# Group 4's second layer in seven products, three load buffers in turn, and late spreads in a score bank

## The chip, the cores and the metric

The kernel runs on one NeuronCore of a Trainium2 chip. The metric is device time in microseconds (us) of one execution; the profile's own times start at the first instruction of the span. Engines are called by their names: TensorE (PE in the profile) multiplies matrices, VectorE (DVE), ScalarE (ACT) and GpSimd (POOL) do elementwise work, and SyncE (SP) issues most of the transfers. 16 DMA engines move the data.

## The reference

Two steps are computed, over a batch of 8, 8 heads, 576 positions and a head width of 64. First a Nystrom attention with 32 landmarks for each head, then a two-layer network on the 512 channels with its own normalization.

```python
q_lm, k_lm = means of q and k over 18 neighbouring positions     # 32 landmarks
A, Bm, C = softmax(q k_lm'), softmax(q_lm k_lm'), softmax(q_lm k')
Z = Bm' / (norm1(Bm) * norminf(Bm));  6 times: Z = 2 Z - Z Bm Z
x = A Z C v                                                      # [8*576, 512]
out = x + relu(normalized(x) * g @ w1) @ w2                      # 512 -> 2048 -> 512
```

The 4608 rows of x make 36 blocks of 128, and four blocks make a group, so that the network runs over nine groups of 512 rows (0 to 8).

## The kernel before, in words

**Two streams on TensorE.** The attention goes batch by batch: first batches 0 and 1, then four sets, (2), (3, 4), (5, 6) and (7). Each set is a `Coming` object (L510), which loads q, k and v by units of four heads into staging buffers, casts them to fp16 on GpSimd, turns them on VectorE and adds up landmarks. `attention2` (L660) is a generator with a yield after each step: scores of k, products with v, six iterations for Z, and then the rows, one block of x each. The network is another generator, `mlp` (L958). `fill(n)` (L1046) advances it by n yields, so n matmuls of 512 columns, or n pairs of matmuls of 256 columns. The plan `steps` (L1150) holds for each attention step of each set how many yields of the network follow it, how many casts, and how many preparation jobs (a turn, a landmark sum, or a spread) of the next set. The loop at L1155 carries this out. Every engine keeps the order in which the program issues its instructions, so an instruction that waits holds up those behind it on its engine. That is true of SyncE's queue of transfers as well.

**Normalization.** When a block of x is complete, `block_done` (L746) has its mean formed, its squares summed on ScalarE (`square`, one per attention step) and the block centred on GpSimd (`center`, L789), then turned by a transposing transfer into xnT, which the first layer reads. For groups below `G_FAST` (L45, 5) only the mean is taken off before the first layer, and 1/deviation is applied at the end, on VectorE, with the sum of x and the second layer in a buffer `ot`. For groups from `G_FAST` on, 1/deviation is applied before the first layer (`normalize`, L773, block by block), so that the second layer's result can be added straight to x.

**Second layer.** Below `G_FAST`, each of a group's four blocks takes sixteen matmuls of 512 columns into one bank. From `G_FAST` on, the 512 x 2048 by 2048 x 512 product is cut into 2 x 2 parts and done in seven products (Winograd's form of Strassen's) of sixteen matmuls with 256 columns each (`second_layer`, L870). It needs four mixes of w2's parts (`mixes_of_w2`, L857, on GpSimd) and four of the hidden layer's parts (`mix_of_h`, L946, and one inside `second_layer`, on VectorE). The first product is copied out by ScalarE and added three times by GpSimd; the others are collected two to a bank and added to x by VectorE.

**Buffers.** The staging pool `stage` (L58) has six buffers that are handed out in rotation to the loads; the four w2 mixes and two h mixes take all six once the loads are done. PSUM pools are `ps1` (one bank: iterations and small products), `ps2` (two buffers for scores, products with v, and rows) and `psM` (three banks: the network, and the landmark spreads psl of sets before batch 7). `mout` (L253) has four output buffers `ot`.

`prepare` (L1111) keeps three loads staged and not yet cast: after each cast it issues the next load. In set (2), step 9, three further loads are issued.

Of the kernel before, what the change touches and what calls it, by code (L numbers as in the profile page):

```python
# [16 lines left out]
P = 128  # L17
# [3 lines left out]
def kernel(  # L21
# [23 lines left out]
    G_FAST = 5  # L45
# [36 lines left out]
    def load(src, b, u, queue):  # L82
        t = stage.tile([P, 2, NJ, D], FP32, name="stg", tag="stg")
        keep(queue.dma_start(
            out=t[:],
            in_=src[b, 4 * u:4 * u + 4].rearrange("(r e) (t j) d -> (e t) r j d", e=2, j=NJ)))
        return t
# [14 lines left out]
    def load_turned(src, b, u, queue):  # L102
        t = stage.tile([P, 2, NJ, D], FP32, name="stg", tag="stg")
        rows = src[b, 4 * u:4 * u + 4].rearrange("(r e) (t j) d -> e t r j d", e=2, j=NJ)
        for half in range(2):
            keep(queue.dma_start(out=t[ts(half, 64), :, :, :], in_=rows[1 - half]))
        return t
# [401 lines left out]

    class Coming:  # L510
# [31 lines left out]
        def load(self, i, queue=nc.sync):  # L542
            nm, w = self.parts[i]
            b, u = self.units[w]
            src = {"q": q, "k": k, "v": v}[nm]
            self.stg[i] = (load_turned if nm == "v" and u % 2 == 1 else load)(src, b, u, queue)
# [54 lines left out]
        def spread(self, y):  # L601
            part = self.part.pop(y)
            late = self.bs[0] >= 7
            psl = (ps1 if late else psM).tile([P, 2, 8, LM], FP32, name="psl",
                                              tag="p1" if late else "pm")
            for half in range(2):
                MM(psl[:, half, :, :].rearrange("p k c -> p (k c)"),
                   spread16[:, half, :, :, :].rearrange("p e a w -> p (e a w)"),
                   part[:].rearrange("p n w r l x -> p (n w r l x)"))
            lm = asm.tile([P, 8, 2, LM], FP16, name="lm", tag="lm", bufs=3)  # L610
            scalar.copy(lm[:].rearrange("p k h c -> p h k c"), psl[:])
            for i, nm in enumerate(("q", "k")):
                for x in range(2):
                    self.lm[nm, 2 * y + x] = lm[:, ds(4 * i + 2 * x, 2), :, :].rearrange(
                        "p r h (l x) -> p r (h l) x", x=2)
# [130 lines left out]
    def block_done(j):  # L746
        g, u = divmod(j, 4)
        if g >= G_FAST:
            mean_of(j, dve)
            squares.append((at[0] + -4, lambda: normalize(j)))  # L750
            return
        if g == 0:
            mean_of(j, dve)
            center(j, scalar if u % 2 == 0 else dve)
        elif g == 1:
            mean_of(j, dve)
            later.append(lambda: center(j, scalar))
        else:
            later.append(lambda: mean_of(j, pool))
            later.append(lambda: center_in_turn(j))  # L760
        squares.append((at[0], lambda: square(j)))
        if u == 3:
            if g == 1:
                later.append(lambda: ln_ready.add(1))
            squares.append((at[0], lambda: deviations(g)))
# [7 lines left out]
    def normalize(j):  # L773
        g, u = divmod(j, 4)
        square(j)
        if u == 0:
            lnvs[g] = mstat.tile([P, 4], FP32, name="lnv", tag="lnv")
            rstds[g] = mstat.tile([P, 4], FP32, name="rstd", tag="rstd")
        act(lnvs[g][:, u:u + 1], variances[g][:, u:u + 1], AF.Ln, bias=eps_ln[:],
            scale=1.0 / DM)  # L780
        act(rstds[g][:, u:u + 1], lnvs[g][:, u:u + 1], AF.Exp, scale=-0.5)
        center_in_turn(j)
# [70 lines left out]
    w2_mix, h_mix = [], []  # L853
# [3 lines left out]
    def mixes_of_w2():  # L857
        for i in range(4):
            w2_mix.append(stage.tile([P, HK, HN], FP16, name=f"w2mix{i}", tag="stg"))
        for i in range(2):  # L860
            h_mix.append(stage.tile([P, HK, HN], FP16, name=f"hmix{i}", tag="stg"))
        t1, t2, t3, t4 = [t[:] for t in w2_mix]
        for o, a, b, op in ((t1, w12, w11, ALU.subtract), (t3, w22, w12, ALU.subtract),
                            (t2, t3, w11, ALU.add), (t4, w21, t2, ALU.subtract)):
# [4 lines left out]

    def second_layer(g, hT, mixed):  # L870
        t1, t2, t3, t4 = [t[:] for t in w2_mix]
        h11, h12 = hT[:, 0:HK, 0:256], hT[:, HK:MCH, 0:256]
        h21, h22 = hT[:, 0:HK, 256:], hT[:, HK:MCH, 256:]
        s1, s2, s3, s4 = mixed
        x = [x_blk.pop(4 * g + u) for u in range(4)]

# [3 lines left out]
        last = g == NGRP - 1  # L880

        def product(to, left, right, first=True, by_k=False):
            order = [(i, k) for i in range(2) for k in range(HK)]
            if by_k:
                order = [(i, k) for k in range(HK) for i in range(2)]
            for n, (i, k) in enumerate(order):
                apart = isinstance(to, list)
                MM(to[i][:] if apart else to[:, i, :], left[:, k, ts(i, P)], right[:, k, :],
                   start=first and (n == 0 or apart and k == 0), stop=k == HK - 1, skip=True)
                if n % 2 == 1 and n < 15:  # L890
                    yield True

        def add(engine, half, col, t, us=(0, 1)):
            for i in us:
                o = x[2 * half + i][:, ts(col, HN)]
                engine.tensor_tensor(out=o, in0=t[i][:] if isinstance(t, list) else t[:, i, :],
                                     in1=o, op=ALU.add)

        pa = bank("psp1")
        yield from product(pa, h11, w11)  # L900
        p1 = mout.tile([P, 2, HN], FP32, name="p1", tag="ot")
        scalar.copy(p1[:], pa[:])
        for half, col in ((0, 1), (1, 1), (1, 0)):
            add(pool, half, col, p1)
        yield True
        pb = bank("psp6")
        yield from product(pb, s2, t2, by_k=True)
        add(dve, 0, 1, pb)
        yield True
        yield from product(pa, h12, w21, False)  # L910
        add(dve, 0, 0, pa)
# [3 lines left out]
        for k in range(0, HK, 4):  # L915
            dve.tensor_tensor(out=s4[:, k:k + 4, :], in0=h12[:, k:k + 4, :],
                              in1=s2[:, k:k + 4, :], op=ALU.subtract)
        yield True
        yield from product(pb, s3, t3, False)
        add(dve, 1, 1, pb)  # L920
        yield True
        pc = ([psM.tile([P, HN], FP32, name="psp5", tag="pm"),
               ps1.tile([P, HN], FP32, name="psp5", tag="p1")] if last else bank("psp5"))
        yield from product(pc, s1, t1)
        add(dve, 1, 1, pc)
        yield True
        yield from product(pb, h22, t4, False)
        add(dve, 1, 0, pb)
        for u in (2, 3):
            store(4 * g + u, x[u], ts(0, DM), last)  # L930
        yield True
        c = product(pc, s4, w22, False)
# [3 lines left out]
        if last:  # L936
            add(dve, 0, 1, pc, (0,))
            store(4 * g, x[0], ts(1, HN), True)
        for _ in c:
            yield True  # L940
        add(dve, 0, 1, pc, (1,) if last else (0, 1))
# [4 lines left out]
    def mix_of_h(hT, mixed, m):  # L946
        s1, s2, s3, _ = mixed
        h11, h21, h22 = hT[:, 0:HK, 0:256], hT[:, 0:HK, 256:], hT[:, HK:MCH, 256:]
        k0, k1 = {11: (0, 4), 13: (4, 6), 14: (6, 7), 15: (7, 8)}[m]
        n = ds(k0, k1 - k0)  # L950
        dve.tensor_tensor(out=s1[:, n, :], in0=h21[:, n, :], in1=h22[:, n, :], op=ALU.add)
        dve.tensor_tensor(out=s2[:, n, :], in0=s1[:, n, :], in1=h11[:, n, :], op=ALU.subtract)
        if m == MCH - 1:
            for k in range(0, HK, 4):
                dve.tensor_tensor(out=s3[:, k:k + 4, :], in0=h11[:, k:k + 4, :],
                                  in1=h21[:, k:k + 4, :], op=ALU.subtract)

    def mlp():  # L958
        for g in range(NGRP):
# [18 lines left out]
            else:  # L978
# [11 lines left out]
                for m in range(MCH):  # L990
# [7 lines left out]
                    if g >= G_FAST:  # L998
                        if m == 0:
                            while not h_mix:  # L1000
                                yield False
                            mixed = [h[:] for h in h_mix] + [hT[:, 0:HK, 256:],
                                                             hT[:, HK:MCH, 0:256]]
                        if m - 1 in (11, 13):
                            mix_of_h(hT, mixed, m - 1)
                        elif m == MCH - 1:
                            mix_of_h(hT, mixed, 14)
                            mix_of_h(hT, mixed, 15)
# [127 lines left out]
    n = 0  # L1136
# [15 lines left out]
    steps += [[(12, 1, 0), (14, 1, 1), (16, 1, 1), (16, 1, 1)] + 6 * [(9, 1, 1)] + [(10, 1, 1)] + 10 * [(8, 1, 1)]]  # L1152
    steps += [[(15, 0, 0), (18, 0, 0)] + 6 * [(12, 0, 0)] + [(12, 0, 0)] + 5 * [(12, 0, 0)]]
    mixing = mixes_of_w2()
    for c, after, plan in zip(sets, sets[1:] + [None], steps):  # L1155
        while c.jobs:
            prepare(c, 1, 1)
            fill(5 if c is sets[1] else 8)
        for n, ((count, casts, jobs), _) in enumerate(zip(plan, attention2(c.bs, c))):
            for _ in range({(2, 9): 3}.get((c.bs[0], n), 0)):  # L1160
# [6 lines left out]
            if c in sets[2:] and not sets[-1].casts:  # L1167
# [39 lines left out]
```

## Time and profile before

| what | value |
|---|---|
| median of three runs | 319.52 us (317.84 to 319.77) |
| profiled execution, its own time | 318.94 us |
| its span | 317.2 us |
| mean granted TensorE clock | 0.991 |
| TensorE busy | 305.1 us (96%) |
| VectorE, ScalarE, GpSimd busy | 179.0, 161.0, 161.4 us |
| DMA engines' mean share by the core's loads and stores (queue q1) | 54.4% |
| time from issue to landing of a q load (median) | 7.4 us |

The profile is of one execution. In it a matmul's end is modelled, so that consecutive matmuls overlap in the timeline; the chain of waits and the starts give their pace. "idle before <- releaser" in brackets behind an instruction is the time that its engine stood still before it and what ended this; "issue" means that nothing in the profile ended it. In a row of busy times by stretch, each engine has its busy time and the number of its instructions, then come the granted clock (1.00 is full), the DMA share and GB/s. In names, psh is the first layer, pso a second layer in the plain form, psp one in seven products, psec and psea scores, pscv products with v, psn an iteration, psl a spread, psy a row block.

### The profile page before, as it was taken

How to read it: one execution, taken by the hardware profiler on the slowest of the kernel's cores; microseconds unless marked ns; L12 is line 12 of the kernel's file. 1: busy time of each engine (PE TensorE's matmuls, PEld its weight loads, DVE VectorE, ACT ScalarE, POOL GpSimd, SP SyncE). 2: the span in 40 equal slices, each digit the busy share in tenths (PEclk: the TensorE clock that was granted, in tenths of full speed). 3: DMA queues.
4: the chain of work that ended last, by engine and by line, in shares of the span. 5: the costliest groups of instructions: out<-in, count | busy, mean ns of one | idle time of the engine just before them, and what ended most of it. 6: DMA issues, size and time to landing. Idle time of an engine off the chain costs nothing.

```text
span 317.2 us, 8388 instructions
## 1 busy us (share of the span) xinstructions
PE 305.1 (96%) x3424; PEld 173.3 (55%) x3424; DVE 179.0 (56%) x487; ACT 161.0 (51%) x329; POOL 161.4 (51%) x218
## 2 busy tenths in 40 slices
PE   7889999999999979999999999999999999999994
PEld 7557764443444434544454445445854784685583
DVE  3667239868695215899276337756634860561372
ACT  3476853479227741267536646776038706505600
POOL 4389878919995794573003938900900360040050
PEclk9999999999999989999999999999999999999998
DMA  7999999779997994571087004340054016005013
GB/s 278 390 388 386 387 389 264 258 206 333 214 290 156 390 226 107 105 243 28 3 222 174 0 2 90 71 76 0 3 118 83 0 31 154 19 0 132 2 25 110
DMA packets 38862, 50.35 MB, mean 159 GB/s; under 512 B 17572, under 2 KB 18088, under 8 KB 38824
## 3 DMA queue, kind: packets, MB, share of 16 engines
q1 hardware_dynamic: 38504, 49.43, 54.4%
q8 instruction: 27, 0.44, 0.6%
q10 hardware_dynamic: 320, 0.39, 0.4%
q14 instruction: 11, 0.09, 0.1%
HBM read 36.70 MB, written 9.44 MB: 145 GB/s over the span
## 4 chain that ended last, share of the span: by engine, by line
PE 80%; DVE 8%; DMA 7%; issue 2%; POOL 1%; SPq 0%; ACT 0%; DVEq 0%
PE psh L75 39%; PE pso L75 16%; PE psp L75 16%; DMA stg<-in_k_dram 5%; DVE part L69 3%; DMA wstg<-in_moe_w_ch_dram 2%; PE psy L75 2%; PE psn L75 2%; DVE xblk L69 2%; PE pscv L75 2%; DVE xT L69 1%; DVE ot L69 1%; PE psec L75 1%; PE psea L75 1%; PE psl L75 0%
## 5 line engine op out<-in xcount | busy, mean ns | idle before, releaser
L75 PE MATMUL psh<-xnT,w 128*128 128x512 f16 (+1 forms) x640 | 136.2, 360 | 0.1
L69 ACT ACTIVATE hT<-psh 128x512 f16<-128x512 f32 x144 | 84.3, 599 | 78.1 <-PE psh L75 77.6
L75 PEld LDWEIGHTS <-w 128*128 128x128 f16 x640 | 59.0, 98 | 57.3 <-issue 4.2
L75 PEld LDWEIGHTS <-hT 128*128 128x128 f16 x640 | 61.2, 98 | 35.5 <-issue 2.1
L75 PE MATMUL pso<-w,hT 128*128 128x512 f16 x320 | 77.2, 382 | 0.0
L69 POOL TENSOR_TENSOR xblk<-p,xblk 128x256 f32<-128x256 f32 x24 | 17.3, 758 | 62.4 <-ACT p L69 62.4
L69 POOL CAST nat<-stg 128x1152 f16<-128x1152 f32 x28 | 31.6, 1148 | 14.8 <-DMA stg<-in_q_dram 13.2
L69 ACT ACTIVATE junk<-xblk,negm 128x512 f16<-128x512 f32 x36 | 25.9, 719 | 21.4 <-POOL negm L69 13.8
L69 POOL TENSOR_SCALAR xn<-xblk,negm,rstd 128x512 f16<-128x512 f32 x16 | 13.6, 859 | 43.8 <-ACT rstd L69 34.6
L69 DVE SCALAR_TENSOR_TENSOR xblk<-psy,rcpd 128x512 f32<-128x512 f32 (+1 forms) x40 | 27.6, 691 | 1.8
L69 DVE SCALAR_TENSOR_TENSOR st<-st,psn 128x128 f16<-128x128 f16 (+2 forms) x36 | 11.4, 316 | 30.0 <-PE psn L75 30.0
L69 DVE TENSOR_TENSOR xblk<-psp,xblk 128x256 f32<-128x256 f32 x48 | 18.2, 418 | 16.2 <-PE psp L75 16.1
L75 PE MATMUL psp<-w,hT 128*128 128x256 f16 x192 | 23.4, 273 | 0.0
L69 POOL CAST natv<-stg 128x1152 f16<-128x1152 f32 x16 | 18.3, 1164 | 7.4 <-DMA stg<-in_v_dram 7.2
L69 DVE TENSOR_TENSOR hmix<-hT 128x256 f16<-128x256 f16 (+2 forms) x16 | 6.8, 424 | 25.6 <-ACT hT L69 25.5
L69 DVE STREAM_TRANSPOSE xT<-nat 128x576 uint32<-128x576 uint32 x24 | 18.5, 769 | 0.0
L69 DVE TENSOR_REDUCE part<-xT 128x32 f16<-128x576 f16 x26 | 18.3, 744 | 0.1
L69 DVE SCALAR_TENSOR_TENSOR ot<-pso,rstd,xblk 128x512 f32<-128x512 f32 x20 | 14.9, 747 | 5.2 <-PE pso L75 5.0
L69 DVE RECIPROCAL rcpd<-psy 128x8 f32<-128x8 f32 (+1 forms) x40 | 8.1, 202 | 16.5 <-PE psy L75 16.0
L75 PE MATMUL psy<-zcbd,ea 128*128 128x260 f16 (+1 forms) x80 | 15.6, 276 | 0.7 <-DVE zcbd L69 0.5
L75 PE MATMUL psp<-w2mix,hT 128*128 128x256 f16 x128 | 15.5, 273 | 0.0
L75 PE MATMUL psp<-w2mix,hmix 128*128 128x256 f16 x128 | 15.3, 273 | 0.0
(116 smaller groups left out, 324.2 us busy)
## 6 DMA issues: line engine op xcount, KB each, us to landing
stg<-in_q_dram SPq DMA_DIRECT2D x16, 576.0 KB, 7.4
stg<-in_k_dram SPq DMA_DIRECT2D x16, 576.0 KB, 7.3
wstg<-in_moe_w_ch_dram SPq DMA_DIRECT2D x16, 512.0 KB, 7.0
stg<-in_v_dram SPq DMA_DIRECT2D x10, 576.0 KB, 8.9
out_dram<-ot SPq DMA_DIRECT2D x40, 128.0 KB, 2.7
stg<-in_v_dram SPq DMA_DIRECT2D x12, 288.0 KB, 10.8
out_dram<-xblk SPq DMA_DIRECT2D x26, 128.0 KB, 2.3
xnT<-xn SPq DMA_TRANSPOSE x28, 2.5
```

The source lines that it names most:

```text
L69: return lambda *args, **kw: keep(getattr(self.engine, op)(*args, **kw))
L75: keep(nc.tensor.matmul(o, l, r, start=start, stop=stop, tile_position=(rb, cb), skip_group_check=(skip or cb != 0)))
```

## The change

`G_FAST` becomes 4, so group 4 is normalized before its first layer and its second layer takes seven products as well. Its means are formed on GpSimd.

The seven products are put in another order, with three banks. The first product is no longer copied out: VectorE adds it from its bank (pa), then the product with s2 is collected on top of it, added to x, and the product with h21 on top of these, added to x twice. The second product has bank pe, which is used again for the fifth; the third and the last share bank pc. In group 4 the second reading of pa is a copy by ScalarE, added by GpSimd.

The first w2 mix is formed in place in w12, by VectorE, in group 4's first layer; three mixes are left on GpSimd, started in set (3, 4), step 16, and then one piece of two chunks per attention step. Two of the h mixes are formed in place in the hidden layer; the other two lie in the four output buffers, in halves.

Loads of sets (5, 6) and (7) go to three fixed staging buffers in turn. Spreads of these sets use a score bank of `ps2`. Groups 4, 6, 7 and 8 take their deviations together, after the fourth square, and are then centred; group 5 block by block as before.

In the plan, set (2) issues two further loads at step 9 instead of three. Before set (3, 4), each preparation job is followed by six yields instead of five. In set (5, 6), an iteration is followed by six instead of nine, the step after it by eight instead of ten, and each row by twelve instead of eight.

```diff
-    G_FAST = 5
+    G_FAST = 4
...
-    def load(src, b, u, queue):
-        t = stage.tile([P, 2, NJ, D], FP32, name="stg", tag="stg")
+    def load(src, b, u, queue, t=None):
+        t = t or stage.tile([P, 2, NJ, D], FP32, name="stg", tag="stg")
...
+            t = None
+            if self.bs[0] >= 5:
+                if len(ring) < 3:
+                    ring.append(stage.tile([P, 2, NJ, D], FP32, name="ring", tag="stg"))
+                    ring_at[0] = len(ring) - 1
+                t = ring[ring_at[0]]
+                ring_at[0] = (ring_at[0] + 1) % 3
+            self.stg[i] = (load_turned if nm == "v" and u % 2 == 1 else load)(
+                src, b, u, queue, t)
...
-            late = self.bs[0] >= 7
-            psl = (ps1 if late else psM).tile([P, 2, 8, LM], FP32, name="psl",
-                                              tag="p1" if late else "pm")
+            late = self.bs[0] >= 5
+            psl = (ps2 if late else psM).tile([P, 2, 8, LM], FP32, name="psl",
+                                              tag="p2" if late else "pm")
...
         if g >= G_FAST:
+            if g in (4,):
+                later.append(lambda: mean_of(j, pool))
+                squares.append((at[0], lambda: normalize(j)))
+                return
...
         square(j)
+        if g not in (5,):
+            if u == 3:
+                deviations(g)
+                for i in range(j - 3, j + 1):
+                    center_in_turn(i)
+            return
...
+    def last_mix_of_w2(k):
+        dve.tensor_tensor(out=w12[:, k:k + 2, :], in0=w12[:, k:k + 2, :],
+                           in1=w11[:, k:k + 2, :], op=ALU.subtract)
...
+        pa = bank("pspa")
         yield from product(pa, h11, w11)
+        add(0, 0, pa)
         yield True
+        pe = bank("pspe")
+        yield from product(pe, h12, w21)
+        add(0, 0, pe)
+        mix_less(h12, s2)
         yield True
+        pc = ([psM.tile([P, HN], FP32, name="pspc", tag="pm")[:],
+               ps1.tile([P, HN], FP32, name="pspc", tag="p1")[:]] if last else bank("pspc"))
+        yield from product(pc, s1, t1)
+        add(1, 1, pc)
+        yield True
+        yield from product(pa, s2, t2, False)
+        if g in (4,):
+            p6 = mout.tile([P, 2, HN], FP32, name="p6", tag="ot")
+            scalar.copy(p6[:], pa[:])
+            add(0, 1, p6, engine=pool)
+        else:
+            add(0, 1, pa)
+        yield True
+        yield from product(pe, h22, t4)
+        add(1, 0, pe)
...
+        yield from product(pa, h21, t3, False)
+        for u in (0, 1):
+            add(1, 1, pa, (u,))
+            add(1, 0, pa, (u,))
+            store(4 * g + 2 + u, x[2 + u], ts(0, DM), last)
         yield True
-        c = product(pc, s4, w22, False)
+        c = product(pc, h12, w22, False)
...
-                        if m - 1 in (11, 13):
-                            mix_of_h(hT, mixed, m - 1)
-                        elif m == MCH - 1:
-                            mix_of_h(hT, mixed, 14)
-                            mix_of_h(hT, mixed, 15)
+                            mixed = [[mout.tile([P, HK // 2, HN], FP16, name="hmix", tag="ot")[:]
+                                      for _ in range(2)] for _ in range(2)]
+                        if g == G_FAST and m in (2, 4, 6, 8):
+                            last_mix_of_w2(m - 2)
+                        if m in (12, 14, 15):
+                            mix_of_h(hT, mixed, m)
...
-    steps += [[(12, 1, 0), (14, 1, 1), (16, 1, 1), (16, 1, 1)] + 6 * [(9, 1, 1)] + [(10, 1, 1)] + 10 * [(8, 1, 1)]]
+    steps += [[(12, 1, 0), (14, 1, 1), (16, 1, 1), (16, 1, 1)] + 6 * [(6, 1, 1)] + [(8, 1, 1)] + 10 * [(12, 1, 1)]]
...
-            fill(5 if c is sets[1] else 8)
+            fill(6 if c is sets[1] else 8)
...
-            for _ in range({(2, 9): 3}.get((c.bs[0], n), 0)):
+            for _ in range({(2, 9): 2}.get((c.bs[0], n), 0)):
...
-            if c in sets[2:] and not sets[-1].casts:
+            if (c.bs[0], n) >= (3, 16):
```

## The prediction

> **What bounds the kernel now.** I read the page's first part, then the busy times by stretch, the waits of TensorE, and its timeline.
>
> ```profile
> PE 305.1 (96%) x3424; PEld 173.3 (55%) x3424; DVE 179.0 (56%) x487; ACT 161.0 (51%) x329; POOL 161.4 (51%) x218
> ```
>
> TensorE is the bound; the others are half idle. From 60 us to the end of the last product, its waits are only these (who, in us, times, longest):
>
> ```profile
> PE psn L75 <- issue: 1.8, 1, 1.8
> PE psl L75 <- DVE part L69: 0.9, 1, 0.9
> PE psn L75 <- ACT lm L69: 0.7, 1, 0.7
> ```
>
> So a change can gain only by giving TensorE less work or by removing these three stops. The chain of waits gives the price of the work: after 260 us it is TensorE alone, a first layer (psh) and a second layer in seven products (psp), in turn (start, length):
>
> ```profile
> 260.70 13.81 PE psh L75 x64
> 274.52 12.23 PE psp L75 x112
> ```
>
> A matmul of 512 columns takes 13.81/64 = 0.216 us, one of 256 columns 12.23/112 = 0.109 us. The largest stop is odd: it falls inside a group of sixteen psn matmuls that are all ready, and slow matmuls follow it (timeline of TensorE; busy times by stretch: PE busy and count, clock, DMA share, GB/s).
>
> ```profile
> 113.36 1.25 PE L75 MATMUL psh<-xnT,w 128*128 128x512 f16 x5
> 114.54 0.23 PE L75 MATMUL psn<-st 32*32 32x64 f16 x5
> 116.53 0.26 PE L75 MATMUL psn<-st 32*32 32x64 f16 x11 [1.76 <-issue]
> 116.72 2.05 PE L75 MATMUL psh<-xnT,w 128*128 128x512 f16 x5
> ```
> ```profile
> 106.00:114.00 8.00, 8.00 (x179) 1.00 1.06 331
> 114.00:116.00 2.00, 0.77 (x8) 1.00 1.01 266
> 116.00:118.00 2.00, 1.47 (x15) 0.76 1.08 205
> 118.00:120.00 2.00, 2.00 (x21) 0.50 1.01 221
> 120.00:122.00 2.00, 2.00 (x25) 0.89 0.83 194
> 122.00:124.00 2.00, 2.00 (x26) 1.00 0.06 22
> ```
>
> The stop comes while the DMA engines are full. Six loads of 576 KB (for batches 5 and 6, unit 1 of q to unit 0 of v; below q1, v0 and so on) are issued between 99.8 and 103.4 us; loads issued then land after 4.6 to 11.8 us. The instructions' DMA queue, which the page calls q8, moves a packet of 16 KB starting near 99.3, 106.3, 113.8, 121.0 and 130.5 us: never closer than 7 us while the queue is full, and TensorE resumes after the one at 113.8 (33.5% of 16 engines in a quarter of a us, so over a us long). I read the stop as TensorE out of instructions behind queued loads.
>
> [...]
>
> **The change, part by part.** The profiled execution took 318.94 us (span 317.2 and 1.7 around it), 0.58 below the median of 319.52; the sum is made on 318.94.
>
> A. Group 4's second layer: 64 matmuls of 0.216 (13.81) become 112 of 0.109 (12.23). All on the path: **-1.58**. The other groups keep 112.
>
> B. Three load buffers in turn. The six buffers let SyncE run up to six loads ahead. With three, load n waits for the cast of load n-3. Following Pool with its own rows (cast 1.15, sums after each q cast 3.0): q1, k2, k3 go out near 100, q2 near 104, then one load each 1 to 4 us, the last (k0 of batch 7) near 120 instead of 112. One to three are queued instead of six, and Pool has cast v1 near 120 (before: 121.3), since Pool, not the transfers, then sets the pace. [...] and TensorE not run dry. The stop is 1.76; the slow clock costs 0.81 (psh x5: 1.99 instead of 1.18), 0.10 (psn) and 0.67 (pso x5: 1.85 instead of 1.18). Between 0 (engines still full) and -3.3; I take **-3.3**. SyncE's waits: behind the waiting loads stand store 8 and the transposes of block 13, not ready before 124.
>
> C. Six matmuls instead of five in each of seven turns before (3,4)'s scores. DVE is busy without a gap from 88 to 95.7 there, and TensorE waits 0.92 at psl. Six more matmuls before psl are 1.3: **-0.9** (between -0.9 and 0).
>
> D. Landmark spreads move to the score banks: the psn that waited for the copy of psl out of the single ps1 bank loses its wait, **-0.7**. The score banks are free for over 1 us at those places.
>
> E. Group 4's normalization moves: the four blocks are centred together after their deviations at step 0 of (5,6), and xnT 16 to 19 follow there. From the first psec of (5,6), counted as zero: ACT's exponentials end at 2.3, square and deviations at 3.5, four centres of 0.77 on Pool at 6.7; SyncE issues store 13 (1.1) at 4.2 and four transposes of 1.22, the last at 9, landed (2.8) at 11.7. TensorE wants them after 44 psh/pso matmuls (9.5), psec, gram and two pscv (3.2): 12.7. Hidden with 1 us of cover; **+0.1** (0 to 2).
>
> F. Mixes of w2: twelve on Pool instead of sixteen, started at step 16 of (3,4), so that they (1.12 each) stand between batch 7's casts. By the same clock, Pool reaches the end of q1's cast and sums at 22.0. DVE reaches the turn of q1 near 21, at its end of step 6, and waits; behind it stand st of iteration 3 and the sums of spread 7. The iterations are also packed tighter, six matmuls (1.3) instead of nine (1.95) between them. TensorE wants psl at 22.7 and st at 22.9, and gets st at about 23.8: **+1.0** (0 to 2).
>
> G. Group 3's first layer now begins one step earlier. After psy 15 come DVE's row, Pool's mean and centre (2.4), then SyncE, busy with store 9 and xnT 14 until 2.9; a transpose there takes 3.7 to 4.4 to land (127 to 131 us). So xnT 15 is there at 6.6 to 7.3, and TensorE, after 27 matmuls and four psy, at 6.7: **+0.3** (0 to 1).
>
> H. Adds. Each of groups 5 to 8 had twelve DVE adds of 128x256 (0.418) and six on Pool (0.76); now sixteen on DVE. In group 4, two go over ACT and Pool. No product reads a mix sooner than two products (3.5) after its last input, and mixes end about 2 after it; in-place mixes save nothing on the path. But four adds (1.67) now stand behind the third collection in pa, against one product (1.75) until the next group's first psh takes that bank; in group 4, rows (1.15 a block) are queued between. **+0.3** over four groups (0 to 1). The last mix of w12, four of 0.42 on DVE, has half-idle DVE as cover and joins F if that is gone.
>
> I. The end. In the last group the same four adds push the two last ones and their stores: the last add ended 0.6 after its product, now about 1.0: **+0.45** (0.2 to 0.8).
>
> Sum: -1.58 - 3.3 - 0.9 - 0.7 + 0.1 + 1.0 + 0.3 + 0.3 + 0.45 = **-4.3**, so 314.6 on the profile's execution and 315.2 from the median. I say **314.9**. What is late next: TensorE again, everywhere.
>
> **Rivals.** (1) *B gives nothing*: ten loads still have to pass between 100 and 122, the engines stay full, and TensorE runs dry there or a page later. For: DMA share is 1.0 throughout this stretch, also when fewer loads are queued. Against: q8's gap opens with the number queued. Then -1.0: 317.9 to 318.5, no change. Chance 0.20.
>
> (2) *The three buffers pace Pool* (slower). If a load lands 4.6 or later even with two queued, each of the ten loads costs about 3.5 instead of 2.3; v1's cast moves from 121 to 133. Pool's centres 13 to 15 and SyncE's transposes stand behind it, xnT 15 lands near 140, and the first layer of group 3 is wanted near 131.5. TensorE then stands for 8, the gains of 6.5 are gone, and with the other losses it ends at 321 to 322. It decides as soon as v1 is cast 5 later than now. For: no slack in order on Pool. Against: the loads landed late because six were queued; 390 GB/s is 1.5 us for one. Chance 0.14.
>
> (3) *Group 4's inputs or DVE's queue are later than in E and F*: cover of 1 us is thin, since the landing alone varies from 2.4 to 5.6. Both at their far ends, +3: 317.5. Chance 0.14.
>
> **How the numbers follow.** The forecast, with 0.52, is 312.4 (no losses) to 316.4. What a measurement of this kernel can tell from no change is 1%, here 3.2: below 316.3. Faster: 0.50 of the forecast and 0.04 of rival 3 and 0.03 of a partial B; same: 0.02, 0.09 and 0.17; slower: 0.14, and 0.01 of rival 3. So 0.57, 0.28, 0.15. The range leaves out rival 2 and a little of each end: 312.2 to 319.3.
>
> **What would show it.** A: 112 psp for group 4, over 12.2 us. B: no "issue" row above 1 us and a clock of 1.00 from 100 to 122; loads landing in 3 to 6. C, D: no psl or psn row. E, G: a row psh <- DMA xnT if wrong. F: psl or psn <- DVE behind a Pool cast. I: the last DVE add 1.0 after the last product. I am wrong if Pool's cast of v1 is later than 126, or if the stop returns at another page.

## The result and the profile after

The changed kernel has a median of 314.65 us (six executions, 313.92 to 316.13) against 318.45 for the kernel before beside it: a ratio of 0.988, with an interval of 0.984 to 0.991. Eleven later executions gave 315.2 (E8 below). The forecast was 314.9. Executions over 1.5% longer than the shortest of their kernel are set aside in all ratios and differences of this text: 26 of 87 of the kernel before beside the experiments (321.1 to 328.2) and one of its six here, three of 17 in E5, and no other; what they lost was not profiled.

The profiled execution is the longest of the six (316.13, span 314.4, clock 0.999). The page's first part shows TensorE with as large a share of the span as before, and more matmuls (48 more, group 4's):

```profile
PE 302.9 (96%) x3472; PEld 178.6 (57%) x3472; DVE 192.9 (61%) x529; ACT 156.2 (50%) x308; POOL 141.3 (45%) x192
```

The waits of TensorE from 60 us to the end (who, in us, times, longest) are four, and none of the three of before is among them at its old size:

```profile
PE psh L75 <- DMA xnT<-xn: 0.7, 1, 0.7
PE pspa L75 <- DVE xblk L69: 0.4, 1, 0.4
PE pspa L75 <- ACT p L69: 0.3, 1, 0.3
PE psl L75 <- DVE ot L69: 0.2, 1, 0.2
```

The iteration in which TensorE had stopped for 1.76 us is the last line here (timeline of TensorE), without a stop, and the stretches around it have the clock at 1.00 (stretch, its length, TensorE's busy time and count, clock, DMA share, GB/s):

```profile
115.55 0.30 PE L75 MATMUL psn<-st 32*32 32x64 f16 x16
115.78 0.82 PE L75 MATMUL psh<-xnT,w 128*128 128x512 f16 x3
116.44 0.59 PE L75 MATMUL pso<-w,hT 128*128 128x512 f16 x2
116.96 0.29 PE L75 MATMUL psn<-st 32*32 32x64 f16 x16
```
```profile
106.00:114.00 8.00, 8.00 (x197) 1.00 0.51 142
114.00:116.00 2.00, 2.00 (x47) 1.00 1.01 393
116.00:118.00 2.00, 2.00 (x25) 1.00 1.09 263
118.00:120.00 2.00, 2.00 (x41) 1.00 0.87 166
120.00:122.00 2.00, 2.00 (x34) 1.00 0.73 240
```

The reader should see two things: from 106 to 114 the DMA engines are now half idle (0.51, before 1.06), and TensorE has no idle time in any of these rows, with the engines full from 114 to 118 as before. The end is as before, TensorE alone, in 64 first-layer matmuls and seven products (chain of waits: start, length):

```profile
283.70 13.81 PE psh L75 x64
297.52 1.75 PE pspa L75 x16
299.26 1.75 PE pspe L75 x16
```

Where the time went, between these two profiles: from the last row of set (2), the first half of block 13 (psy at 86.38 before, 87.55 after), to the start of the last product (310.88 and 307.83) is 224.50 before and 220.28 after, 4.2 less; to the end of the span it is 4.0 less. The profiled execution of the changed kernel reaches that row 1.2 later, though nothing in TensorE's program is changed up to there (its small waits in the first 60 us are longer: 1.0 instead of 0.5 at psn, 0.6 instead of 0.2 at psxt). The spans therefore differ by only 2.8.

One thing has to be said on the size: the 61 executions of the kernel before that the comparisons below use lie between 315.7 and 320.8, and the 40 among them with a granted clock of 0.997 or more have a median of 317.7, the other 21 one of 319.7, so that the stop with its slow clock, as the profile of before shows it, is probably not in every execution. Of the 17 executions of the changed kernel, two have a clock below 0.997.

### The profile page after: what moved, and what is told of

It is laid out like the page before. It is cut to its first block, busy times and chain, and to the rows that moved or that the text cites. A ratio compares the mean times of both kernels' runs of the same rounds, so it can differ in the third digit from the quotient of the medians.

```text
span 314.4 us, 8482 instructions
## 1 busy us (share of the span) xinstructions
PE 302.9 (96%) x3472; PEld 178.6 (57%) x3472; DVE 192.9 (61%) x529; ACT 156.2 (50%) x308; POOL 141.3 (45%) x192
## 4 chain that ended last, share of the span: by engine, by line
PE 66%; DVE 13%; issue 8%; POOL 7%; DMA 2%; ACT 2%; SPq 0%; POOLq 0%; ACTq 0%; DVEq 0%
PE psh L75 33%; PE pspa L75 7%; PE pso L75 7%; PE pspe L75 5%; PE pspc L75 4%; DVE xblk L69 3%; DVE part L69 3%; POOL w2mix L69 2%; DMA stg<-in_k_dram 2%; PE psy L75 2%; PE psn L75 2%; DVE ot L69 2%; DVE xT L69 2%; POOL asum L69 2%; POOL nat L69 1%
## 5 line engine op out<-in xcount | busy, mean ns | idle before, releaser
L75 PE MATMUL pso<-w,hT 128*128 128x512 f16 x256 | 61.3, 380 | 0.0
L69 POOL TENSOR_SCALAR xn<-xblk,negm,rstd 128x512 f16<-128x512 f32 x20 | 16.3, 825 | 78.5 <-DVE hmix L69 40.8
L69 POOL CAST nat<-stg 128x1152 f16<-128x1152 f32 x16 | 18.1, 1145 | 10.6 <-DMA stg<-in_q_dram 8.7
L69 DVE TENSOR_TENSOR xblk<-pspa,xblk 128x256 f32<-128x256 f32 x38 | 13.8, 416 | 5.4 <-PE pspa L75 5.4
L75 PEld LDWEIGHTS <-hmix 128*128 128x128 f16 x160 | 15.5, 98 | 2.6 <-DVE xblk L69 0.7
L69 DVE SCALAR_TENSOR_TENSOR ot<-pso,rstd,xblk 128x512 f32<-128x512 f32 x16 | 11.9, 746 | 7.0 <-PE pso L75 6.9
L69 POOL CAST nat<-ring 128x1152 f16<-128x1152 f32 x12 | 13.6, 1144 | 5.2 <-DMA ring<-in_q_dram 5.2
L69 POOL CAST natv<-stg 128x1152 f16<-128x1152 f32 x10 | 11.4, 1162 | 7.8 <-DMA stg<-in_v_dram 7.8
L75 PEld LDWEIGHTS <-st 32*32 32x32 f16 x448 | 5.7, 90 | 15.3 <-issue 8.9
L69 POOL TENSOR_TENSOR asum<-asum 128x256 f32<-128x256 f32 (+1 forms) x22 | 13.0, 593 | 1.7
```

The costliest lines, as they stand in the source:

```text
L69: return lambda *args, **kw: keep(getattr(self.engine, op)(*args, **kw))
L75: keep(nc.tensor.matmul(o, l, r, start=start, stop=stop, tile_position=(rb, cb), skip_group_check=(skip or cb != 0)))
```

## The experiments

**E1. The three buffers alone.** Before, with only the loads of sets (5, 6) and (7) in three buffers in turn.

```diff
...
+            if self.bs[0] >= 5:
+                if len(ring) < 3:
+                    ring.append(stage.tile([P, 2, NJ, D], FP32, name="ring", tag="stg"))
+                    ring_at[0] = len(ring) - 1
+                t = ring[ring_at[0]]
+                ring_at[0] = (ring_at[0] + 1) % 3
...
```

> The kernel before, with only the three load buffers in turn for batches 5 to 7. Theory (TensorE starved of instructions behind queued loads): no row with "issue" above 1 us after 100 us and a clock of 1.00 from 98 to 122; packets of the instruction queue about 5 us apart there instead of 7; the stops at psl (0.9) and at the psn behind the copy of psl (0.7) stay; 3.3 less than before, less up to 0.7 for a later xnT: 315.5 to 316.5, ratio 0.988 to 0.991. Rival (the engines stay full, B gives nothing, and the stop went for another reason): the stop stays or moves, ratio 0.998 to 1.002. Rival (the buffers pace GpSimd): a wait of psh for xnT of several us, ratio above 1.

Measured: 318.07 (seven executions), ratio 0.994 (0.990 to 0.999), 1.9 less by the ratio and 1.6 by the medians (319.69 before), where 3.3 was expected. The waits of TensorE from 60 us on:

```profile
PE psh L75 <- DMA xnT<-xn: 1.7, 1, 1.7
PE psl L75 <- DVE part L69: 0.8, 2, 0.5
PE psn L75 <- ACT lm L69: 0.7, 1, 0.7
```

The stop for instructions is gone, with nothing else changed. In its place stands a wait for the transposes of group 2, whose landing took 4.0 to 7.1 us here, with the third load of set (2), step 9, just ahead of them on SyncE. That wait has its own slow clock behind it (same columns as above):

```profile
97.00:99.00 2.00, 0.93 (x4) 0.89 1.08 313
99.00:101.00 2.00, 2.00 (x51) 0.50 0.87 194
101.00:103.00 2.00, 2.00 (x40) 0.76 0.61 120
```

So in this execution the buffers do what step B says, and it pays the same kind of price some 18 us earlier. The instruction packets on q8 follow: in the kernel before they start at 99.4, 106.3, 113.8 and 121.1, in E1 at 101.3, 107.8, 112.7 and 119.0, in the changed kernel at 101.4, 106.4, 110.9 and 117.5. The gaps are 6.9 to 7.5 us before, 4.9 to 6.5 in E1 and 4.5 to 6.6 in the changed kernel.

**E2. Forty matmuls more, ahead of the plan.** If the stop is a block of instructions that has not arrived, then its place is fixed by the count of instructions and not by what they do. Forty matmuls of 8 columns, whose result nothing reads, are put in front of the plan in the kernel before.

```diff
     fill(18)
+    warm(40, 8)
...
```

> The kernel before, with forty matmuls of 8 empty columns (80 instructions with their weight loads) issued after the last fill before the sets, near 62 us. Theory: the stop comes where a block of 256 instructions ends, so it moves 40 matmuls back in TensorE's order: from after the fifth psn of iteration 3 to about 8 matmuls before the end of the 32 psea of iteration 1, that is near 112 us, with "issue" as its end. Rival (the psn waits for something that the profile doesn't show): it stays at the psn of iteration 3. The forty cost 1 to 2 us by themselves.

Measured (one execution): 321.5. Timeline of TensorE, with two stops now:

```profile
107.23 0.57 PE L75 MATMUL pscv<-natv,ecT 64*32 64x65 f16 x50
109.96 0.28 PE L75 MATMUL pscv<-natv,ecT 64*32 64x65 f16 x22 [2.17 <-issue]
...
116.72 0.45 PE L75 MATMUL psea<-xT,lm 32*32 32x288 f16 x20
117.53 0.32 PE L75 MATMUL psea<-xT,lm 32*32 32x288 f16 x8 [0.36 <-issue]
```

The old stop, inside the sixteen psn of an iteration, is now ahead of the last eight psea of an earlier iteration, and it is short. From there to the old place are 8 psea, 6 psh, 16 psn, 5 psh and 5 psn, which is 40: the stop has kept its count and let the work move by. In front of it a second one, of 2.17, stands inside a group of pscv that are all ready. From it to the second are 22 pscv, 12 psh, 16 psn, 32 psea, 6 psh, 16 psn and 24 psea, 128 matmuls, that is 256 instructions of TensorE, since each matmul has its weight load (3424 of each in the kernel before). The packets of q8 agree in size: the page of the kernel before has 27 of them, 0.44 MB, so one for every 254 of its 6848 matmuls and weight loads. TensorE stood 2.17 and 0.36 for the two blocks, and 1.76 in the kernel before.

**E3. Loads added to the changed kernel.** Three transfers of 512 KB in small pieces (256 bytes), which nothing reads, issued by ScalarE in set (3, 4), step 2, into the buffers that the w2 mixes take later.

```diff
...
+            t = stage.tile([P, HK, HN], FP16, name=f"w2mix{i}", tag="stg")[:]
+            extra.append(t)
+            keep(nc.scalar.dma_start(
+                out=t.rearrange("p k d -> p (k d)").bitcast(FP32)
+                .rearrange("p (m d) -> p m d", d=64),
+                in_=moe_w_ch2[:, ts(i, 64)].rearrange("(p m) d -> p m d", m=MCH)))
...
+            if (c.bs[0], n) == (3, 2):
+                extra_loads()
```

> The changed kernel, with three transfers of 512 KB in pieces of 256 bytes added, issued by ScalarE at step 2 of (3, 4), near 105 us, into the three staging buffers that the w2 mixes overwrite from 134 us on; nothing waits for them but those mixes. Theory: a queue of transfers alone is enough. The instruction packet that came near 110.5 us comes 4 us later or more, a stop of 1 to 4 us with "issue" appears among the iterations near 115 us, and the clock falls below 1 after it; 2 to 6 us slower than the changed kernel. Rival (the rotation of six buffers, or SyncE's waits, made the stop): no stop, under 1 us slower.

Measured (one execution): 323.35. The longest waits of TensorE from 60 us on:

```profile
PE psh L75 <- ACT hT L69: 7.6, 1, 7.6
PE psl L75 <- DVE part L69: 0.5, 1, 0.5
```

TensorE stood 7.6 us for ScalarE, which was held up in issuing the three transfers (8.8 us, from 105.20). The gap between instruction packets opened to 14 us (106.7 to 120.6), but TensorE, standing still, needed none. So the run doesn't tell whether queued loads alone bring the stop back, and is inconclusive. E1 is the better evidence.

**E4. Group 4's second layer in the plain form.** The changed kernel without its first part, for step A.

```diff
-    G_FAST = 4
+    G_FAST = 5
```

> The changed kernel with G_FAST back at 5: group 4 in the plain form (64 matmuls of 512 columns, VectorE into ot), everything else as changed. Theory: 1.58 more matmul time, but the two stops inside group 4's products (0.41 and 0.33) and its part of VectorE's queue go: 0.8 to 1.6 slower than the changed kernel, ratio to before about 0.991. Rival (group 4's seven products give back what they save): same as the changed kernel, ratio 0.988.

Measured: 318.6 (eleven executions), ratio 1.001 (0.997 to 1.006): 3.3 to 4.3 more than the changed kernel by its two ratios, where 0.8 to 1.6 was expected and 1.58 was the price of the matmuls. The longest waits from 60 us on:

```profile
PE pspa L75 <- DVE xblk L69: 1.8, 2, 1.4
PE pscv L75 <- issue: 0.7, 1, 0.7
PE psl L75 <- DVE part L69: 0.5, 1, 0.5
```

Group 4's plain second layer is 64 matmuls, so 64 yields; in seven products, it is 56 yields of two matmuls. Eight more yields move all that follows against the attention's steps. Group 6's products meet batch 7's rows at other points, and their adds stand behind rows and mixes in DVE's queue (0.35 at 250.96 and 1.41 at 256.24); a stop for instructions is back at 165 us, beside batch 7's loads (0.7). These 2.5 stand where the changed kernel has 0.74 of pspa waits, 1.8 more, and with 1.58 that makes 3.4. That this is the reason is argued from the plan and not tested. So this run doesn't price A alone: the plan of the changed kernel is fitted to group 4's 56 yields. What A costs is read from the profile after: the seven products of group 4 run at 0.109 a matmul like all others, apart from the two pspa waits (0.74).

**E5 to E8** stand beside 318.23 for the kernel before.

**E5. Three loads ahead instead of two** in set (2), step 9, in the changed kernel.

```diff
-            for _ in range({(2, 9): 2}.get((c.bs[0], n), 0)):
+            for _ in range({(2, 9): 3}.get((c.bs[0], n), 0)):
```

> The changed kernel, with three loads again instead of two at step 9 of set (2), so that the third stands ahead of the transposes of blocks 9 to 11 on SyncE and the DMA engines. Theory, from the run with the three buffers alone, where psh waited 1.7 for xnT near 96 us and the clock fell after it: xnT 9 to 11 land 1 to 2 us later, psh waits 0.5 to 2 for xnT there, and with the slow clock 1 to 3.5 us are lost; ratio 0.991 to 0.998. Rival (that wait came from fewer matmuls before the first psh of group 2, five instead of six per turn): no wait, ratio 0.988.

Measured: 316.0 (17 executions, 314.58 to 320.43), ratio 0.993 (0.990 to 0.995). That is 0.7 above the changed kernel (E8), without the three of the 17 that took 319.5 or more. The ratio is what the theory said, but the profiled execution (314.58, the shortest) has no wait for xnT, as the rival said. What delays the longer ones was not profiled, so that this stays open.

**E6. Before, with the three buffers, the two loads and the six yields** (B and C; the buffers as in E1).

```diff
...
+            if self.bs[0] >= 5:
...
-            fill(5 if c is sets[1] else 8)
+            fill(6 if c is sets[1] else 8)
-            for _ in range({(2, 9): 3}.get((c.bs[0], n), 0)):
+            for _ in range({(2, 9): 2}.get((c.bs[0], n), 0)):
```

> The kernel before, with three parts of the change: the three load buffers in turn, two loads instead of three at step 9 of set (2), and six matmuls per turn instead of five. Theory: no stop with issue, no wait of psh for xnT near 96, psl's 0.9 gone, psn behind the copy of psl (0.7) left: 3.3 to 4.2 less, up to 0.7 lost at the first layer of group 3; ratio 0.988 to 0.991. Rival (the gain is in the seven products and the order of banks): 0.996 to 1.000.

Measured: 317.05 (22 executions, 315.41 to 319.05), ratio 0.997 (0.995 to 0.999). That is about a third or less of the gain that the theory expected, and within the range of its rival, that the gain is in the seven products and the order of banks. The longest waits from 60 us on:

```profile
PE psh L75 <- DMA xnT<-xn: 1.4, 2, 0.8
PE pscv L75 <- issue: 0.8, 1, 0.8
PE psn L75 <- ACT lm L69: 0.7, 1, 0.7
```

The clock is 1.00 from 98 to 122, but waits of 1.4 for transposes (0.75 at 96, 0.62 at 134) have come in with the three buffers, and a stop for instructions, 0.8, elsewhere. By the medians this is 1.2 less than before, by the ratio 1.0. The rest of the change is then worth 1.85, since E8 is at 315.2: A and D are 2.28 by the prediction, H costs 0.74 by the profile after, which leaves 1.54. So over the executions B and C, whose steps promise 4.2, bring only about a third of E8's gain of 3.0. The stops of 1.4 and 0.8 in E6's own profile, an execution 1.1 longer than its median, may be part of the reason.

**E7. The changed kernel, reordered.** Three waits that the profile after shows (pspa twice, psh for xnT) are attacked. The second half of the mix for h21 goes behind the add of the first product, where DVE has time; the other mix goes behind the adds of pc; and in the plan four yields move from the middle of set (3, 4) to its rows.

```diff
+        dve.tensor_tensor(out=h21[:, 4:8, :], in0=h11[:, 4:8, :], in1=h21[:, 4:8, :],
+                          op=ALU.subtract)
...
-        mix_less(h12, s2)
...
         add(1, 1, pc)
+        mix_less(h12, s2)
...
-        for k in {14: (0,), 15: (4,)}.get(m, ()):
+        for k in {14: (0,)}.get(m, ()):
...
-    steps += [[(6, 1, 0), (8, 1, 0), (12, 1, 0), (12, 1, 0), (6, 1, 0), (6, 1, 0)] + 4 * [(5, 1, 0)] + [(8, 0, 0)] + 3 * [(6, 0, 0)] + 7 * [(7, 1, 1)]]
+    steps += [[(6, 1, 0), (8, 1, 0), (12, 1, 0), (12, 1, 0), (6, 1, 0), (6, 1, 0)] + 4 * [(4, 1, 0)] + [(8, 0, 0)] + 3 * [(6, 0, 0)] + 4 * [(8, 1, 1)] + 3 * [(7, 1, 1)]]
```

> The changed kernel with three moves. On VectorE, the second half of the h21 mix goes behind the first add and the h12 mix behind the add of the third product, so that the adds which free bank pa aren't queued behind mixes; in the plan of (3, 4), iterations have four yields instead of five and the first four jobs' rows eight instead of seven, so that TensorE comes to group 3's first layer 0.9 later after psy 15, at the same count afterwards. Theory: the waits of pspa for VectorE (0.41) and ScalarE (0.33) and of psh for xnT (0.71) go: 0.8 to 1.5 less than the changed kernel, ratio 0.983 to 0.986. Rival (they are covered by something as late): same as the changed kernel in the same call, within 0.002.

Measured: 313.75 (six executions, 313.24 to 316.1), ratio 0.987 (0.981 to 0.993), 1.45 below E8 by the medians. Its profiled execution was its longest. It has none of the pspa waits nor the one at 134, but one near 97 and a stop for instructions of 0.6:

```profile
PE psh L75 <- DMA xnT<-xn: 1.7, 1, 1.7
PE psea L75 <- issue: 0.6, 1, 0.6
PE psl L75 <- DVE part L69: 0.5, 1, 0.5
```

**E8. The changed kernel again**, as it is.

> The changed kernel as it is, beside the others on the same chip: ratio 0.985 to 0.991, no stop with issue between 98 and 122 us.

Measured: 315.2 (eleven executions, 314.48 to 315.92), ratio 0.991 (0.988 to 0.994). Its profile (span 313.1) has both pspa waits (0.4 and 0.3) once more, and no wait for xnT. So H's price is in both profiles of this kernel, G's in one.

**E9 to E11** stand beside 318.22 for the kernel before.

**E9. C and D undone** in the changed kernel.

```diff
-            late = self.bs[0] >= 5
-            psl = (ps2 if late else psM).tile([P, 2, 8, LM], FP32, name="psl",
-                                              tag="p2" if late else "pm")
+            late = self.bs[0] >= 7
+            psl = (ps1 if late else psM).tile([P, 2, 8, LM], FP32, name="psl",
+                                              tag="p1" if late else "pm")
...
-            fill(6 if c is sets[1] else 8)
+            fill(5 if c is sets[1] else 8)
```

> The changed kernel with five instead of six matmuls after each preparation job before set (3, 4), and with the spreads back in the first layer's banks (in ps1 for batch 7): steps C and D undone. By C and D two stops come back, psl <- DVE part of 0.7 to 0.9 near 92 us and psn <- ACT lm of about 0.7, so that the time is 1.0 to 1.6 above the changed kernel's (ratio to before near 0.995). The rival, that the time follows the sum of the matmuls alone and these stops are made good elsewhere, expects no more than 0.3.

Measured: 316.11 (20 executions, 315.43 to 317.04), ratio 0.9933 (0.9911 to 0.9955). Against the ratios of the changed kernel (0.9878 and 0.991) that is 0.7 to 1.75 more, about as C and D say. The timeline of TensorE shows where, in the places named:

```profile
95.95 0.39 PE L75 MATMUL psl<-part,spread 128*128 128x256 f16 x2 [0.39 <-DVE part L69]
...
175.02 0.38 PE L75 MATMUL psl<-part,spread 128*128 128x256 f16 x2 [0.36 <-DVE st L69]
176.07 0.29 PE L75 MATMUL psn<-st 32*32 32x64 f16 x16 [0.67 <-ACT lm L69]
```

D's wait is back to the hundredth (0.67), with one of 0.36 at the psl ahead of it, which neither kernel has. C's is 0.39, not the 0.92 of before: TensorE comes to it at another time. The two pspa waits of group 4 (0.74) are gone, and one of 0.77 stands in group 6 at 253.9 instead: seven yields fewer before the scores move the network here too. So this run doesn't price C and D alone either.

**E10. E7 with the store of block 4 issued by ScalarE**, both halves (SyncE had issued both), so that the two transfers of that store no longer stand between group 2's transposes on SyncE.

```diff
-            (nc.scalar if both and i else nc.sync).dma_start(out=to, in_=half)
+            (nc.scalar if both and i or j == 4 else nc.sync).dma_start(out=to, in_=half)
```

> The reordered kernel with both halves of block 4's store issued by ScalarE instead of one by SyncE, so that the transposes of group 2 stand behind one transfer less on SyncE near 90 us. If the wait psh <- DMA xnT near 96 to 98 us (1.67 in the reordered kernel's profile) comes from the place in SyncE's queue, it goes, and the time falls by 0 to 1 below the reordered kernel's. If it comes from the landing time under the loads alone (5.6 to 6.9 us), it stays at 0.5 to 1.7 and the time is the same within 0.3.

Measured: 314.12 (six executions), ratio 0.986 (0.981 to 0.992). The wait stayed (timeline of TensorE):

```profile
97.61 1.24 PE L75 MATMUL psh<-xnT,w 128*128 128x512 f16 x5 [1.79 <-DMA xnT<-xn]
```

The last transpose of group 2 was issued at 92.2 instead of 93.4 in E7, but took 5.3 to land instead of 4.3, and is there at the same time (97.5 and 97.7). The ones ahead of it took up to 7.9. In this execution the wait comes from the landing under the loads, and not from that place in SyncE's queue alone. One profile of each doesn't settle it, since E11 below, without the move, has no such wait.

**E11. E7 again.**

> The reordered kernel (mix of h21's second half behind the adds of pa, the other mix behind the adds of pc, four more yields moved to the end of set (3, 4)) once more, beside the other two. If it gains by the three waits that it removes (pspa <- DVE 0.4, pspa <- ACT 0.3, psh <- DMA xnT 0.7), it is again 1.0 to 1.5 below the changed kernel's 315.2, at 313.5 to 314.2 (ratio 0.983 to 0.988); if its first figure was chance, it is at 315.

Measured: 313.53 (six executions, 313.22 to 315.57), ratio 0.9865 (0.981 to 0.992). One wait of TensorE is left from 60 us on, and that is at 60.8 us:

```profile
PE psl L75 <- DVE part L69: 0.5, 1, 0.5
```

In E11's profile the last transpose of group 2 was issued at 91.7 (93.4 in E7) and took 3.9, so it was in time. The version of E7 is thus faster than the kernel before, by 4.5 and 4.7 between the medians (E7, E11). It is probably faster than the changed kernel, 0.9 to 1.7 below its medians: four of E7's six executions are shorter than the shortest of E8's eleven (314.48), but two are longer than E8's median, and the intervals of the ratios overlap. That nearly the same figure came twice, and that both profiles lack the pspa waits, is what speaks for it.

## Why the prediction was right, point by point

The forecast (-4.3 on the profile's execution) came out at -4.0 in these two profiles from the last row of set (2) on, at -3.8 and -3.0 by the medians (here and E8), and at -3.9 and -2.9 by their ratios (times 318). Not all of its steps did.

**A** (-1.58) stands by the trace: 112 matmuls at 0.109. As a difference of two kernels it could not be had, since E4 shifts the network against the plan.

**B** (-3.3) was right in its mechanism and at most about half right in its size. E2 shows the stop to be a late block of 256 instructions; E1's profile no longer has it. Since the stop is not in every execution, one profile could miss it by chance, but the two profiles with six load buffers (before, E2) have stops of 1.76 and 2.17, and in the eleven with three buffers the longest stop with "issue" is 0.8 (E6).

The traces say more on the mechanism than E2 alone. Five of the stops with "issue" after 60 us can be counted in the timelines (before, two in E2, E4, E9). Each comes after a count of matmuls that is 93 or 94 above a multiple of 128: 1630 before, 1502 and 1630 in E2, 2141 in E4, 1502 in E9. From 94 on there are 27 such places in the kernel before and in the changed one, and q8 has 27 packets in each. In the profile of before TensorE stands at place 13 (1630 = 94 + 12 x 128) until the 12th packet has landed, at 115.11, and goes on at 116.53, 1.42 us after its end. To each other place n + 1 after 60 us it comes 1.84 us or more after the end of the n-th packet in that profile, and 2.08 or more in the profile after. So in these two profiles TensorE passes a place only when the packet before has landed. That queued loads make the packet late rests on E1 and on the gaps between packets (6.9 to 7.5 us before, 4.9 to 6.5 in E1).

But by the ratios E1 gains 1.9 and E6, with C, 1.0. The step took the stop and slow clock of one profiled execution as the price in all. By the granted clocks, about a third of the executions of before (21 of 61) and two of 17 of the changed kernel have such a loss; that this is the stop near 115 us in each of them is argued, since one alone was profiled. Loads issued between 99 and 125 us landed after 4.6 to 11.8 us before and 4.0 to 7.4 after (3 to 6 was said), and the last went out at 124.7 instead of the 120 that the step counted. Besides, B brought its own price: with three buffers the loads are spread later, between 112 and 133, and meet transposes (G, E1, E6).

**Rival 2** (Pool paced by three buffers) is refuted: v1's cast ended at 123.1 in the profile after, 122.0 without the later start, and it decided at 5 later than 121.3. Pool's waits for loads of q into the three buffers, 5.2 in all, show in no wait of TensorE. **Rival 1** (B gives nothing) is refuted by E1's and the changed kernel's profiles, with a grain left in it: small stops for instructions (0.3 to 0.8) turn up elsewhere in E4, E6, E7 and E9. In the changed kernel the DMA engines were full from 114 to 118 (1.01 and 1.09) without a stop. **Rival 3** did not come.

**C** (-0.9) measured -0.74 in the profile after, its psl wait being 0.18 at 97.5; **D** (-0.7) measured -0.67. E9, with both undone, has a wait at each of the two places again.

**E** (+0.1) cost nothing. The transposes of group 4 went out from 159.2 and the first psh ran at 166.6 without a wait; the cover was 0.1 instead of 1, so this was near.

**F** (+1.0) was too much: psl waited 0.12 (at 177.22) and st not at all. Pool finished q1's sums 22.3 after the step's zero, against 22.0 predicted, but TensorE came at 23.3 instead of 22.7. TensorE's arrival, 0.6 later than counted, is the larger part of what was mis-sized.

**G** (+0.3) measured 0.71 in the profile after (TensorE's timeline):

```profile
134.16 1.67 PE L75 MATMUL psh<-xnT,w 128*128 128x512 f16 x7 [0.71 <-DMA xnT<-xn]
```

After psy 15 (126.34), xnT 15 was issued at 3.3 (the step says 2.9) and there at 7.8 (6.6 to 7.3), and TensorE came at 7.1 (6.7). The trace has no landing for this transpose; by the end of the wait it took about 4.5 us, against 4.4 at most in the step. The transposes of blocks 13 and 14 ahead of it took 6.9 and 5.4: the last v loads of set (5, 6) and the first load of batch 7 are now issued from 122.1 to 124.7, just ahead of them (before, the last load of this stretch at 112.2). The step took its landing time from a profile in which no load was issued there, though B itself had moved loads to it. In E8 xnT 15 landed after 2.4 us and there is no wait: it is chance in part.

**H** (+0.3 over four groups, between groups) was right only in that the adds cost something. It put the waits at the first psh of the next group, which waited in none. They are inside group 4's products, two of them, 0.74 (TensorE's timeline):

```profile
190.70 1.48 PE L75 MATMUL pspa<-w2mix,hmix 128*128 128x256 f16 x12 [0.41 <-DVE xblk L69]
194.92 0.60 PE L75 MATMUL pspa<-w2mix,hT 128*128 128x256 f16 x4 [0.33 <-ACT p L69]
```

The first is the price of one bank read and then collected on: the product with s2 may go on top of pa only after DVE has added it, and this add stood at 189.90 behind the mixes (185.23 to 188.8) and a row, though the first product's matmuls had ended at 186.6. The second is the same with ScalarE's copy, which stood at 194.30 behind the square of a row block that itself waited 2.19 for VectorE. The step asked how long after the product a bank must be free; it did not ask which work stands ahead of the reader on its engine. E7 and E11, which only change this order and the plan, show no pspa wait. Which of the two did it was not tested apart.

**I** (+0.45): the last add ended at 310.21 and 313.24, both 0.6 after the last product. The four adds at pa's end fit (308.03 to 309.45) while the last product runs. Span after the last add is 4.2 against 4.0, so +0.2. The step's end, 1.0 after the last product, did not come.

The steps up to the last product, as measured in these two profiles, are -1.58 (A), -3.3 (B, in this execution), -0.74, -0.67, 0.12 (F), 0.71 (G), 0.74 (H): -4.7, against -4.2 there. 0.5 stays unassigned. F, G and H together cost what was predicted (1.57 against 1.6), but in other shares. Over the executions B is worth 1.0 to 1.9 less instead of 3.3, F costs 0.1 instead of 1.0, and G, absent in E8, less than its 0.7. So the hit of the figure is in part luck: errors of opposite sign.

## What to carry to other kernels

When an engine stops among instructions that are all ready, count instructions from the start of the program: if the stop stays at a fixed count when work is put in front (in E2 two stops, 256 instructions apart), ask whether the instructions had arrived (before, TensorE went on 1.42 us after a packet of q8 had ended). What helped here was fewer loads queued at that moment (E1, no stop for instructions in its profile) rather than any change of the work there. A wait's price is that of one execution; take as much of it as the spread of the times allows. And for a bank that is read and then collected on again, follow the reader's own queue: not when the product ends, but what stands ahead of the add.

## What the runs showed of the hardware

TensorE stood up to 2.17 us for one block of instructions while loads were queued (E2, DMA share 1.05 from 107 to 110). A stop can cost more than itself: 1.76 in the kernel before and 2.17 in E2 were followed by 0.76, 0.50, 0.89 and by 0.77, 0.50, 0.88 of the clock over six us, and the rows around the wait of 1.71 in E1 have 0.89, 0.50 and 0.76. In the kernel before, the clock stood at 0.50 for 3.41 us, from 117.03. For E2 and E1 I estimate 3.4 us at 0.50, from what their three rows of 2 us lack of the full clock (together 0.85 of a row, 1.7 us, in each). But stops of 1.67 (E7) and 1.79 (E10) were followed by nothing (busy times of E7 by stretch):

```profile
97.00:99.00 2.00, 1.28 (x7) 1.00 0.99 244
99.00:101.00 2.00, 2.00 (x56) 1.00 1.02 393
101.00:103.00 2.00, 2.00 (x58) 1.00 0.92 207
```

E10 has 1.00 from 95 to 103 too. So the length of a stop alone did not decide in these runs, since 1.71 has a slow clock behind it and 1.79 has not; what else decides is not shown by them. Last, a transpose of 128x512 landed after 2.4 us at best in the kernel before, and after up to 7.9 among loads (E10). One that was issued 1.2 earlier (E10 against E7) was there 0.2 earlier.
